# RetNet attention and SwiGLU feed-forward: how the first eight jobs turn q on TensorE

## The chip, the cores and the metric

The kernel runs on one core of one Trainium2 chip. A core has TensorE (PE in the profile, with its weight loads as PEld), VectorE (DVE), ScalarE (ACT), GpSimd (POOL) and SyncE (SP), which here issues nearly all transfers between HBM and SBUF. TensorE reads SBUF and writes PSUM, of which this kernel uses eight banks of 128 partitions by 512 float32 words. The metric is the device time of one execution in microseconds (us), as a median of several.

## The reference, cut to what matters

All data are float32. The first half is retention (linear attention with a decay) for 8 batches of 8 heads, 576 positions and 64 values per head; the second is a normalisation and a SwiGLU feed-forward over the 4608 rows that come out of it.

```python
scores = scale * np.matmul(q, k.transpose(0, 1, 3, 2))
Dmat = np.where(rel >= 0, gamma[:, None, None] ** rel[None, :, :], 0.0)
attn = np.matmul(scores * Dmat[None], v)
x = attn.transpose(0, 2, 1, 3).reshape(B * S, H * D)
xn = x / rms * rms_g
g, val = xn @ w_gate, xn @ w_val
out = (g * (1.0 / (1.0 + np.exp(-g))) * val) @ w_out
```

## The kernel before

**Jobs.** The attention is cut into 32 jobs, a batch and a pair of heads each. A job needs q and k with the 64 head values on the partitions, head 0 of the pair on partitions 0 to 63 and head 1 on 64 to 127, whereas memory has the positions in the rows. Jobs 8 to 31 turn them on VectorE (`prepare`, line 257). Jobs 0 to 7 turn them on TensorE, in the function `turn` (lines 220 to 250), which the change edits.

**What `turn` does.** It works on three PSUM banks. For q, the 512 first positions come as `d["q"]`, 128 partitions by 2 heads by 4 chunks by 64 values. For each of the four chunks and each of the two heads, the 128 by 64 piece is the stationary operand of a matrix product with the 128 by 128 identity `ident` as the moving one (line 234). `side(e)` is partitions 64e to 64e+63, so the product of head 0 lands in the upper half of the bank and that of head 1 in the lower, in every fourth column. For k both heads lie side by side, and a chunk is turned by one `nc.tensor.transpose` of 128 by 128 (line 228). ScalarE then copies each bank to SBUF (`qT`, `kT`, line 239). The 64 last positions of q and k are turned by two more transpositions of 64 by 128 (line 243) and copied too (line 250).

**What follows in a job.** `slot(j)` (line 404) issues on TensorE `values(j-1)` (line 355), `scores(j)` (line 285), `states(j)` (line 305) and `carried(j-1)` (line 375), all in products of 64 rows by 64 columns; on VectorE `weigh` (line 318, `ret`) and `sums` (line 334, `sum`). `states` needs v after `scale_v` on ScalarE (line 266).

**Order.** Every engine runs its own instructions in the order in which the program lists them. For the first part of the kernel that order is written out by hand in a string `PLAN`; `T` is `turn`, `S` is `slot`, `V` is `scale_v`, `Q` and `G` the squares for the normalisation, `N`, `D`, `X` the normalisation itself (`ms` line 454, `diag` line 468, `rb` line 519), `U` a block of the plain up projection of the first two row blocks (line 674), and `w` and `a` steps of a preparation of the weights on VectorE and ScalarE. It begins

```python
PLAN = """
    V0 T0 a1 a1 a1 S0 T1 V1 a1 S1 T2 V2 a1 a1 V3 w1 S2 w1 Q0 T3 Q1 a1 G0 S3 a1 a1 V4 T4 a1
    G1 a1 S4 a1 T5 a1 Q2 w1 G2 V5 w1 V6 Q3 S5 T6 a1 G3 a1 Q4 w1 V7 w1 S6 w1 F8 G4 N0 w1 a1
    a1 D0 a1 T7 w1 a1 a1 a1 a1 X0 S7 ...
```

The loads of these jobs are issued from SP's queue in the order of a list, before everything else: `load_first` (lines 170 and 178) for q, k and v, `load_tails` (line 188) for the last positions, with four blocks of weights among them (line 1034). Jobs 0 to 3 are loaded into the tile `h`, jobs 4 to 7 into `ring`. None of these loads waits for TensorE.

After the jobs of the plan, row blocks 2 to 8 follow in a loop, in which matrix products of the feed-forward (lines 614 and 779) fill TensorE and the remaining jobs are woven in.

Of the kernel before, what the change touches and what calls it, by code (L numbers as in the profile page):

```python
# [14 lines left out]
P = 128  # L15
# [26 lines left out]
def kernel(  # L42
# [11 lines left out]
    nc = tc.nc  # L54
    B, H, S, D = q.shape
# [31 lines left out]
    def bank(name):  # L87
        return banks.tile([P, 512], F32, tag="b", name=name)
# [13 lines left out]
    ident = const.tile([P, P], F32, name="ident")  # L102
# [107 lines left out]
    def warm_up(n, width=P):  # L210

        if not warm_of:
            warm_of[0] = bank("warm")
        for _ in range(n):
            nc.tensor.matmul(
                warm_of[0][:, :width], lhsT=ones, rhs=ones[:, :1].to_broadcast([P, width]),
                start=True, stop=True,
            )

    def turn(j):  # L220

        d = st[j]
        n = NFULL
        for nm in "qk":
            ps = bank(f"turn_{j}_{nm}")
            for c in range(n):
                if nm == "k":
                    nc.tensor.transpose(
                        out=ps[:, c * P : c * P + P],
                        in_=d["k"][:, c].rearrange("p e d -> p (e d)"), identity=ident,  # L230
                    )
                    continue
                for e in range(2):
                    nc.tensor.matmul(
                        ps[side(e), c : n * P : n], lhsT=d["q"][:, e, c], rhs=ident,
                        start=True, stop=True,
                    )
            t = d[nm + "T"] = att.tile([P, S], F32, tag=nm + "T", name=f"{nm}T_{j}")
            nc.scalar.copy(out=t[:, : n * P], in_=ps[:, : n * P])
        last = bank(f"turn_{j}_t")  # L240
        for i, nm in enumerate("qk"):
            o = slice(i * TAIL, i * TAIL + TAIL)
            nc.tensor.transpose(
                out=last[:, o], in_=d[nm + "t"].rearrange("p e d -> p (e d)"),
                identity=ident[:TAIL, :TAIL],
            )
        warm_up(j == 0, 2 * P)
        for i, nm in enumerate("qk"):
            o = slice(i * TAIL, i * TAIL + TAIL)
            nc.scalar.copy(out=d[nm + "T"][:, NFULL * P :], in_=last[:, o])  # L250
# [21 lines left out]
    def side(i):  # L272
        return slice(i * L, i * L + L)
# [922 lines left out]
    def start():  # L1196
# [12 lines left out]
        for i in (1, 0, 2):  # L1209
# [9 lines left out]
        }  # L1219
        tasks = {  # L1220
            "S": lambda j: slot(j, rest=j not in (0, FIRST)), "C": close, "T": turn, "V": scale_v,
            "P": prepare, "F": fetch, "Q": lambda j: squares.append(squared(*divmod(j, NHP))),
            "G": lambda j: gather(*squares.pop(0)), "N": norm_1, "D": diagonals, "X": norm_2,
# [83 lines left out]
```

## Time and profile before

| | us |
|---|---|
| median of 3 runs | 1109.53 |
| lowest and highest of them | 1109.16, 1113.54 |
| the profiled execution, its own time | 1110.56 |
| its span, first to last instruction | 1108.6 |
| TensorE busy in the span | 1090.6 |
| VectorE busy | 794.0 |
| GpSimd busy | 458.0 |
| ScalarE busy | 278.6 |

The profile is of one execution. Its span leaves 1.96 us of its own time outside. A matrix product in float32 is recorded as two instructions with a weight load each; a transposition as one. A line of a timeline has the start, the time from the first start to the last end, engine, line, what is written and read, the size of the stationary operand, the moving data, and a count; in brackets stands idle time ahead of it and what ended that. "issue" is waiting for which the profile shows no reason. The ends of matrix products are modelled, so starts are the safer measure. The eight calls of `turn` lie in the first 60 us, and the first plain up projection starts at 59.37 us.

### The profile page before, as it was taken

Reading aid. Unit: us, or ns where it says so; the run is one execution under the profiler, and the core shown is the slowest. Engines: PE = TensorE matmul, PEld = TensorE weight load, DVE = VectorE, ACT = ScalarE, POOL = GpSimd, SP = SyncE. Lnnn points to the kernel's source line nnn. Section 1 sums busy time; section 2 is a strip of 40 time slices with the busy share of each in tenths; the row PEclk is TensorE's granted clock in tenths of the full one; section 3 lists DMA queues with packets and bytes.
Section 4 is the critical chain, followed back from the end, with each engine's and each line's share of the span. In section 5 each row is a group of like instructions: output and inputs, shape, how many; then the busy total and the mean of one; then the engine's idle time right before and its main releaser. Section 6 shows DMA issues by size and latency. Waiting matters only on the chain.

```text
span 1108.6 us, 24401 instructions
## 1 busy us (share of the span) xinstructions
PE 1090.6 (98%) x10102; PEld 915.3 (83%) x10102; DVE 794.0 (72%) x1379; ACT 278.6 (25%) x565; POOL 458.0 (41%) x421
## 2 busy tenths in 40 slices
PE   8899999999999999999999999999999999999998
PEld 7754444479988899889988898889888998898888
DVE  4788578788867885778668785779476935594466
ACT  4665465211121311122022202131122111211110
POOL 0025335538430286026802482229311941393236
PEclk9899999999999999999999999999999999999999
DMA  7766798597978876897769965998475754585461
GB/s 182 204 198 222 261 267 217 198 342 187 289 269 219 201 262 222 203 230 226 268 191 206 283 251 157 242 240 290 146 207 200 266 204 169 179 288 165 152 247 41
DMA packets 253870, 243.72 MB, mean 220 GB/s; under 512 B 193088, under 2 KB 213824, under 8 KB 247616
## 3 DMA queue, kind: packets, MB, share of 16 engines
q1 hardware_dynamic: 252752, 241.87, 71.1%
q8 instruction: 79, 1.29, 0.5%
q10 hardware_dynamic: 1008, 0.30, 0.1%
q14 instruction: 31, 0.25, 0.1%
HBM read 212.05 MB, written 30.08 MB: 218 GB/s over the span
## 4 chain that ended last, share of the span: by engine, by line
PE 93%; DVE 3%; SPq 1%; ACT 1%; issue 1%; DMA 1%; POOL 0%; POOLq 0%; ACTq 0%; DVEq 0%
PE up L674 15%; PE x L614 13%; PE z L614 13%; PE w L614 13%; PE y L614 7%; PE xo L779 6%; PE xp L779 4%; PE zo L779 4%; PE zp L779 3%; PE yo L779 2%; PE wo L779 2%; PE av L355 2%; PE yp L779 2%; PE wp L779 2%; PE s L285 2%; PE av L375 1%
## 5 line engine op out<-in xcount | busy, mean ns | idle before, releaser
L674 PE MATMUL up<-x,ring 128*128 128x512 f32 x384 | 166.8, 594 | 0.0
L614 PE MATMUL x<-x,ring 128*128 128x256 f32 x672 | 160.8, 382 | 1.0 <-DVE t L698 1.0
L614 PE MATMUL w<-sums,ring 128*128 128x256 f32 x672 | 158.8, 379 | 0.0
L614 PE MATMUL z<-x,ring 128*128 128x256 f32 x672 | 158.7, 379 | 0.0
L736 POOL TENSOR_TENSOR vi<-h 128x384 f32<-128x384 f32 x32 | 39.9, 1248 | 277.0 <-DVE h L633 267.9
L674 PEld LDWEIGHTS up<-x,ring 128*128 128x128 f32 x384 | 72.4, 190 | 88.9 <-issue 85.6
L614 PEld LDWEIGHTS z<-x,ring 128*128 128x128 f32 x672 | 127.7, 190 | 19.9 <-issue 2.9
L614 PEld LDWEIGHTS w<-sums,ring 128*128 128x128 f32 x672 | 127.6, 190 | 17.4
L614 PEld LDWEIGHTS x<-x,ring 128*128 128x128 f32 x672 | 125.5, 190 | 18.2 <-issue 0.9
L741 POOL TENSOR_TENSOR vi<-h 128x384 f32<-128x384 f32 (+2 forms) x46 | 46.9, 1019 | 150.3 <-DVE h L633 150.3
L976 POOL TENSOR_TENSOR vi<-vi 128x512 f32<-128x512 f32 (+1 forms) x77 | 78.1, 1026 | 38.3 <-DVE vi L806 33.3
L640 ACT COPY m<-x 128x512 f32<-128x512 f32 x42 | 24.6, 586 | 230.4 <-PE x L614 230.4
L614 PE MATMUL y<-sums,ring 128*128 128x256 f32 x336 | 79.5, 379 | 1.5 <-DVE sums L533 1.5
L614 PEld LDWEIGHTS y<-sums,ring 128*128 128x128 f32 x336 | 63.7, 190 | 10.6 <-issue 2.0
L621 DVE TENSOR_TENSOR h<-u,w 128x512 f32<-128x512 f32 x42 | 28.9, 688 | 59.2 <-PE w L614 58.9
L621 DVE TENSOR_TENSOR u<-m,y 128x512 f32<-128x512 f32 x42 | 28.7, 684 | 47.9 <-PE y L614 47.8
L635 ACT ACTIVATE h<-h 128x512 f32<-128x512 f32 x63 | 39.7, 630 | 81.7 <-DVE h L621 81.7
L334 DVE SCALAR_TENSOR_TENSOR sum<-sum,gc,s 128x64 f32<-128x64 f32 x192 | 53.9, 281 | 6.8
L1096 POOL TENSOR_TENSOR vi<-vi 128x512 f32<-128x512 f32 (+1 forms) x24 | 40.3, 1681 | 36.9 <-DVE vi L1085 14.8
L741 POOL TENSOR_TENSOR vi<-vi,h 128x384 f32<-128x384 f32 (+2 forms) x46 | 47.9, 1042 | 3.6
L318 DVE SCALAR_TENSOR_TENSOR ret<-s,causal 128x320 f32<-128x320 f32 x64 | 28.5, 484 | 27.4 <-PE s L285 26.8
L1096 POOL TENSOR_TENSOR ring<-ring 128x512 f32<-128x512 f32 x24 | 30.5, 1275 | 42.1 <-DVE ring L1085 35.0
(310 smaller groups left out, 2050.3 us busy)
## 6 DMA issues: line engine op xcount, KB each, us to landing
ring<-w_out_blocks SPq DMA_DIRECT2D x59, 1344.0 KB, 6.6
ring<-w_up_blocks SPq DMA_DIRECT2D x42, 1792.0 KB, 7.9
w_out_blocks<-vi SPq DMA_DIRECT2D x21, 448.0 KB, 6.0
out_dram<-vi SPq DMA_DIRECT2D x64, 128.0 KB, 3.5
qraw<-in_q_dram SPq DMA_DIRECT2D x96, 72.0 KB, 5.2
kraw<-in_k_dram SPq DMA_DIRECT2D x96, 72.0 KB, 3.3
k<-in_k_dram SPq DMA_DIRECT2D x48, 128.0 KB, 3.1
v<-in_v_dram SPq DMA_DIRECT2D x48, 128.0 KB, 3.2
```

The costliest lines, as they stand in the source:

```text
L318: nc.vector.scalar_tensor_tensor(out=ret[:, e], in0=s[e][:, : n * L].rearrange("p (c k) -> p c k", k=L), scalar=float(_gamma(H)[2 * hp + e ...
L334: nc.vector.scalar_tensor_tensor(out=t[:, c], in0=t[:, c - 1], scalar=gc[:, hp : hp + 1], in1=part, op0=ALU.mult, op1=ALU.add,)
L614: nc.tensor.matmul(ps[:, i * HU : i * HU + HU], lhsT=w[:, PLACE[blk], c, i * P : i * P + P], rhs=t_of[u][blk][:, c], start=(start and i == ...
L621: nc.vector.tensor_tensor(out=o, in0=a, in1=pairs_of(ps), op=ALU.add)
L635: nc.scalar.activation(out=o, in_=c, func=AF.Silu)
L640: nc.scalar.copy(out=s1, in_=pairs_of(x_))
L674: nc.tensor.matmul(ps, lhsT=w[:, PLACE[blk], c % 2, i * P : i * P + P], rhs=x_of[u][:, c], start=(c == 0), stop=(c == NHP - 1),)
L736: eng.tensor_tensor(out=i1, in0=x12, in1=x11, op=ALU.subtract)
L741: eng.tensor_tensor(out=o[:, c], in0=a[:, c], in1=b[:, c], op=op)
L779: nc.tensor.matmul(ps, lhsT=lhs[:, c], rhs=w[:, s, c], start=((nm, s // 4) not in first), stop=False, skip_group_check=True,)
L976: eng.tensor_tensor(out=t[:, :, o], in0=t[:, :, x], in1=t[:, :, y], op=ALU.add)
L1096: nc.gpsimd.tensor_tensor(out=t[o], in0=t[x], in1=t[y], op=op)
```

## The change

In `turn`, head 0 of each chunk of q is turned by a transposition that writes partitions 0 to 63 of the bank; head 1 keeps its product with the identity. The order becomes head 0, head 1 for chunk 0, then for chunk 1 and so on, one of each kind in turn. Columns, banks, copies, the k part and the tails are as before, and so is every other function.

```diff
-                for e in range(2):
-                    nc.tensor.matmul(
-                        ps[side(e), c : n * P : n], lhsT=d["q"][:, e, c], rhs=ident,
-                        start=True, stop=True,
-                    )
+                nc.tensor.transpose(
+                    out=ps[:D, c : n * P : n], in_=d["q"][:, 0, c], identity=ident
+                )
+                nc.tensor.matmul(
+                    ps[side(1), c : n * P : n], lhsT=d["q"][:, 1, c], rhs=ident,
+                    start=True, stop=True,
+                )
```

## The prediction

> **What bounds the kernel now.** I read the page first, for the engine that ends last.
>
> ```profile
> PE 1090.6 (98%) x10102; PEld 915.3 (83%) x10102; DVE 794.0 (72%) x1379; ACT 278.6 (25%) x565; POOL 458.0 (41%) x421
> ...
> q8 instruction: 79, 1.29, 0.5%
> ...
> PE 93%; DVE 3%; SPq 1%; ACT 1%; issue 1%; DMA 1%; POOL 0%; POOLq 0%; ACTq 0%; DVEq 0%
> ```
>
> TensorE is busy for 1090.6 of 1108.6 us and makes up 93% of the chain. Of its 18 us of idle time some 10 lie before 59.4 us, where the edited function runs; the waits view after 60 us has about 5 us in all, the longest 1.5 (`y` for `sums`). So a microsecond added to TensorE before 59.4 us reaches the end, unless a wait in that stretch swallows it. Next, which instructions are concerned: the view of the tile `turn_q`, and that of line 228.
>
> ```profile
> L234 PE MATMUL turn_q<-ident,h x64: 272/273/476, 6.1 to 24.2; 128*64 128x128 f32 x64
> L234 PE MATMUL turn_q<-ident,ring x64: 272/273/474, 30.3 to 53.8; 128*64 128x128 f32 x64
> ```
> ```profile
> L228 PE MATMUL turn_k<-ident,h x16: 272/273/476, 8.0 to 24.8; 128*128 128x128 f32 x16
> ```
>
> Four jobs in `h` have 4 chunks x 2 heads = 32 products and 64 records: two passes each. Line 228 has 16 for 16 transpositions: one pass. The durations overlap, so prices come from starts, in the timeline of TensorE:
>
> ```profile
> 6.12 1.98 PE L234 MATMUL turn_q<-ident,h 128*64 128x128 f32 x16 [1.98 <-DMA h<-in_q_dram]
> 8.03 1.12 PE L228 MATMUL turn_k<-ident,h 128*128 128x128 f32 x4
> 9.07 0.47 PE L243 MATMUL turn_t<-ident,vi 64*128 64x64 f32 x2
> ...
> 12.41 1.09 PE L234 MATMUL turn_q<-ident,h 128*64 128x128 f32 x16
> 13.44 0.65 PE L228 MATMUL turn_k<-ident,h 128*128 128x128 f32 x4
> 14.02 0.34 PE L243 MATMUL turn_t<-ident,vi 64*128 64x64 f32 x2
> ...
> 30.31 0.62 PE L234 MATMUL turn_q<-ident,ring 128*64 128x128 f32 x6 [1.37 <-DVE sum L334]
> 33.20 1.54 PE L234 MATMUL turn_q<-ident,ring 128*64 128x128 f32 x10 [2.27 <-issue]
> ```
>
> The same view cut at 12.58 and at 12.69 us:
>
> ```profile
> 12.41 0.44 PE L234 MATMUL turn_q<-ident,h 128*64 128x128 f32 x4
> 12.41 0.55 PE L234 MATMUL turn_q<-ident,h 128*64 128x128 f32 x6
> ```
>
> Two more passes, one of each head, take one step of p = 0.11 us. So the heads' passes run side by side, and 16 passes are 8 steps. The q part takes 13.44 - 12.41 = 1.03 = 8p + 0.15, the k part 14.02 - 13.44 = 0.58 = 4p + 0.14. What is over, s = 0.145 us, is paid once at the end of each part, where the shape of the tile changes (128x64, 128x128, then 64x128). Within a part it isn't paid. In job 0 the same two equations, 1.91 = 8p + s and 1.04 = 4p + s, give p = 0.2175 and s = 0.17: half the clock.
>
> **What the Trainium skill says.** TensorEngine Tiling (Array Packing), Key Properties: "Changing tiling mode (not just tile) drains the TensorE", and tiles of one mode run in parallel. The trace agrees on both: s, and the two heads in one step. The same page, Gotcha 2: column tiling excludes the transpose mode for float32 input. So a transposition, though of 64 columns, takes the whole array. No instruction before is of this form, so the trace can't confirm it. TensorE: Matmul & The Clock Gate, Part 1: half clock until a window of about 3.4 us was busy, and again after an idle one. The trace agrees (0.2175 against 0.11), and the windows view shows a second such phase:
>
> ```profile
> 5.00:8.40 3.40, 2.28 (x18) 1.98 (x19) 0.00 (x0) 0.09 (x1) 0.00 (x0) 1.00 0.97 244
> 8.40:11.90 3.50, 3.50 (x52) 2.33 (x54) 0.00 (x0) 2.46 (x8) 0.00 (x0) 1.00 1.12 224
> 28.90:32.30 3.40, 0.66 (x8) 0.41 (x6) 3.11 (x11) 0.61 (x1) 0.00 (x0) 1.00 0.69 149
> 32.30:35.80 3.50, 2.60 (x15) 1.94 (x16) 0.00 (x0) 1.97 (x5) 0.00 (x0) 0.51 0.76 178
> 35.80:39.20 3.40, 3.40 (x113) 3.28 (x115) 0.49 (x1) 2.83 (x6) 0.09 (x1) 0.51 0.86 204
> ```
>
> Columns: stretch, length, busy PE, PEld, DVE, ACT, POOL, granted clock, DMA. (The clock's record begins at 11.9 us, so 1.00 ahead of it means nothing.) After 0.66 us of work in a window the clock halves at 32.3; after 2.60 of 3.50 it stays down; after a full window it returns at 39.2. Perfetto Trace Analysis, Transposes, advises transpositions over ordinary products; it says nothing of mixing them.
>
> **The change, part by part.** *Passes.* Per chunk, head 0 goes from two passes to one. That alone saves nothing: head 1 still needs two, and they set the length of the chunk, 2p. *Order.* Now transposition (whole array) and product (128x64) alternate, so each chunk has two changes of mode, and nothing lies beside anything: p + s + 2p + s = 3 x 0.11 + 2 x 0.145 = 0.62 us, four chunks 2.48 against 1.03. **+1.45 us per job** at full clock (the last s is the one paid now at the exit). At half clock 3 x 0.2175 + 2 x 0.17 = 0.99, four 3.97 against 1.91: **+2.06**. The bounds of this unseen mixture: 0 if the narrow transposition runs in the 128x64 mode, +1.45 if every change drains. I take the upper. ScalarE's copy of `turn_q` starts later by the same amount; behind it in ScalarE's queue wait the copy of `turn_k` and the scaling of v, and for these TensorE's scores and states, which shift with TensorE anyway. No DMA, bank or VectorE instruction is added.
>
> *Along the path.* Job 0: +2.06. It also puts drains into the window from 8.4 to 11.9, where now TensorE is busy throughout. Up to 10.2 us the array would stream 3 x 0.2175 of each 0.99, 66%, like the windows that weren't granted the clock (2.28 of 3.40 is 67%, 2.60 of 3.50 74%). I expect the grant one window later, at 15.3: states of job 0 at half clock (about +0.3) and the beginning of the next turn (+0.15). At T1 that is +2.5. Jobs 1 to 3: 3 x 1.45 = 4.35, sum 6.85. Of it waits for v disappear: 0.31 in job 2 (a bracket at 21.81, for ACT `h`), and in job 3 this one, in the chain of waits:
>
> ```profile
> 19.71 4.09 DMA h<-in_v_dram
> ...
> 23.82 0.51 ACT h L266
> ...
> 26.20 0.49 ACT kT L239
> ...
> 26.73 0.84 PE s L285 x39
> ```
>
> TensorE sat idle 0.65 us before 26.73 because ScalarE had waited for v of job 3 until 23.8. SP's loads don't move, so this cover goes once: 6.85 - 0.31 - 0.65 = 5.9 us late in the scores of job 3. VectorE's sums follow the scores and move with them.
>
> *Job 4* is the largest single term, and it has the other sign. Its turn stops at 30.93 for 2.27 us for "issue", and then runs at half clock to 39.2. The stop looks like a missing instruction: one packet of the instruction queue q8 lies between 30.5 and 31.0 us. At 1.29 MB in 79 packets, with 20204 instructions on TensorE, a packet would be 256 of these, somewhat less than a job. With TensorE 5.9 us later and slower in its turns, such a packet has longer to come, and the queue of loads that it shares the DMA engines with is shorter. I take the stop away, and the clock with it: 2.48 + 4.13 (a job from its k part to the next turn, 13.44 to 17.57) = 6.61 us where 30.31 to 40.19 was 9.88: -3.27, own drains included. The bounds: -3.27, and +2.06 if stop and half clock stay. Now late by 2.6.
>
> Job 5: +1.45, less a wait of 0.30 for v at 44.32. Job 6: +1.45. Job 7: +1.45, less the 0.64 that TensorE waits at 55.61 for `diag`, which doesn't hang on this turn. Sum 2.6 + 1.15 + 1.45 + 0.8 = **+6.0 us**. VectorE, busy for 6.4 of 6.8 us around 46 to 53, is the next engine in line, but its work resumes with the scores of job 4, less late than TensorE at the end. After 59.4 nothing gives back more than tenths.
>
> 1110.56 + 6.0 = 1116.6 us in the profiled execution's terms. That lies 1.03 above the median of the three runs, which spread over 4.4; I put the forecast at 1116.
>
> **The rivals.** *B: the stop in job 4 stays, or another comes, with half clock behind it.* For it: packets of instructions share the DMA engines with loads, and drains thin the work that keeps the clock up. Against it: the time per instruction grows. 5.9 + 2.06 + 3.4 = +11.4, 1121.5. *C: no change of mode.* The transposition of 64 columns takes the 128x64 tile of head 0 beside head 1's product. Then a chunk stays at 2p, and the only effect is 8 fewer instructions per job, 32 before job 4. Time 1110; if those 32 let the packet come in time, 3.3 less, 1107. It decides at one point: whether the step after a transposition costs p or p + s. Against it stands Gotcha 2. This case isn't slower. *A2: the clock of job 0 is granted at 11.9 as before.* Then jobs 0 and 1 lose 1.5 less, 1114.5.
>
> **How the numbers follow.** About 0.5%, 5.5 us, is what a measurement of this kernel tells from no change: slower begins at 1115.1. My forecast (with A2 as its lower part) 0.57, 1112 to 1119; B 0.28, 1119 to 1125; C 0.15. Slower: all of B and 0.6 of the first, 0.62. Faster: part of C, 0.06. Same: 0.32. The range 1111 to 1123 leaves out C and the end of B.
>
> **What would show it.** Right: q parts of about 2.5 us with 12 passes in warm jobs, starts of a transposition and of the next product about 0.25 apart; no "issue" of 2 us near 35 us; full clock from 15.3 on; the up projection starting near 65.4 instead of 59.37. Wrong: q parts of 1.03 us (C), a stop and a clock of 0.5 past 20 us (B), or a wait of TensorE after 60 us that shrinks by microseconds.

## The result and the profile after

The changed kernel takes 1116.68 us, median of 18 runs (1112.92 to 1121.15), beside 1109.28 us for the kernel before (18 runs, 1105.46 to 1113.54). The ratio is 1.0063, with a 95% interval of 1.0052 to 1.0075: slower by about 7 us. The forecast was 1116.

The profiled execution of the changed kernel took 1119.07 us (span 1117.1), 2.4 us above its median, and that of the kernel before 1110.56, 1.3 above its own. So the two traces differ by 8.5 us. The page after, busy engines and the chain of waits:

```profile
PE 1103.4 (99%) x10070; PEld 918.5 (82%) x10070; DVE 795.1 (71%) x1379; ACT 278.4 (25%) x565; POOL 458.3 (41%) x421
...
PE 96%; DVE 2%; ACT 1%; issue 1%; DMA 0%; POOL 0%; SPq 0%; POOLq 0%; ACTq 0%; DVEq 0%
```

TensorE has 32 records fewer (8 jobs x 4 products that are now one pass), yet is busy for 12.8 us more, and its share of the chain went up. The other engines work as before. The timeline of TensorE in job 2, at full clock, shows why:

```profile
20.59 0.30 PE L233 MATMUL turn_q<-ident,h 128*64 128x128 f32 x1
20.82 0.43 PE L236 MATMUL turn_q<-ident,h 128*64 128x128 f32 x2
21.18 0.30 PE L233 MATMUL turn_q<-ident,h 128*64 128x128 f32 x1
21.41 0.43 PE L236 MATMUL turn_q<-ident,h 128*64 128x128 f32 x2
...
22.96 0.66 PE L228 MATMUL turn_k<-ident,h 128*128 128x128 f32 x4
23.55 0.34 PE L245 MATMUL turn_t<-ident,vi 64*128 64x64 f32 x2
```

Line 233 is the transposition, line 236 the product. One chunk takes 21.18 - 20.59 = 0.59 us, the q part 22.96 - 20.59 = 2.37 (1.03 before), and the k part is as before (0.59; 0.58 before). The q parts alone add 8 x 1.34 = 10.7 us of TensorE time at full clock. The first up projection starts at 67.66 instead of 59.37 us. All but 0.2 us of the 8.5 has been lost by then.

The granted clock, in the windows view (length, busy PE, PEld, DVE, ACT, POOL, clock, DMA):

```profile
7.80:14.60 6.80, 6.80 (x88) 4.35 (x86) 1.40 (x5) 2.55 (x8) 0.00 (x0) 0.50 0.85 174
14.60:41.90 27.30, 25.15 (x636) 18.61 (x635) 17.64 (x60) 15.78 (x40) 0.36 (x4) 1.00 0.95 229
41.90:48.80 6.90, 6.90 (x130) 5.21 (x130) 3.70 (x7) 4.25 (x13) 0.09 (x1) 0.51 0.76 250
...
59.00:65.80 6.80, 6.80 (x70) 3.77 (x72) 3.68 (x7) 6.10 (x14) 0.36 (x2) 0.50 0.66 134
```

Three phases of 6.8 us at half clock, where the record of the kernel before has one (its start, before 11.9 us, is slow too, but outside the record). One follows another stop for "issue", in the `carried` part ahead of job 5:

```profile
37.94 0.91 PE L377 MATMUL av<-qT,sum 64*64 64x64 f32 x24
40.45 0.45 PE L377 MATMUL av<-qT,sum 64*64 64x64 f32 x8 [1.61 <-issue]
```

How late the changed kernel's execution is at each turn, from the starts in the two timelines, beside what the prediction's sum had there:

| start of | before, us | after, us | late by | forecast |
|---|---|---|---|---|
| turn 1 | 12.41 | 13.70 | 1.29 | 2.5 |
| turn 2 | 17.57 | 20.59 | 3.02 | 3.95 |
| turn 3 | 23.36 | 27.15 | 3.79 | 5.1 |
| turn 4 | 30.31 | 33.08 | 2.77 | 5.9 |
| turn 5 | 40.19 | 40.83 | 0.64 | 2.6 |
| turn 6 | 45.87 | 49.63 | 3.76 | 3.75 |
| turn 7 | 52.71 | 57.75 | 5.04 | 5.2 |
| up projection | 59.37 | 67.66 | 8.29 | 6.0 |

The medians fit (1116 forecast, 1116.68 measured), and several rows don't. The experiments ask two things: what makes the q part long, and how much of that length reaches the end.

### The profile page after: what moved, and what is told of

It is laid out like the page before. It is cut to its first block, busy times and chain, and to the rows that moved or that the text cites. A ratio compares the mean times of both kernels' runs of the same rounds, so it can differ in the third digit from the quotient of the medians.

```text
span 1117.1 us, 24332 instructions
## 1 busy us (share of the span) xinstructions
PE 1103.4 (99%) x10070; PEld 918.5 (82%) x10070; DVE 795.1 (71%) x1379; ACT 278.4 (25%) x565; POOL 458.3 (41%) x421
## 3 DMA queue, kind: packets, MB, share of 16 engines
q8 instruction: 79, 1.29, 0.5%
## 4 chain that ended last, share of the span: by engine, by line
PE 96%; DVE 2%; ACT 1%; issue 1%; DMA 0%; POOL 0%; SPq 0%; POOLq 0%; ACTq 0%; DVEq 0%
PE up L676 15%; PE x L616 13%; PE w L616 13%; PE z L616 13%; PE y L616 7%; PE xo L781 6%; PE xp L781 4%; PE zo L781 4%; PE zp L781 3%; PE yo L781 2%; PE wo L781 2%; PE av L357 2%; PE s L287 2%; PE av L377 2%; PE yp L781 2%; PE wp L781 2%
```

## The experiments

Each ratio is to the kernel before on the same chip, with its 95% interval.

### Grouped: four transpositions, then four products

```diff
-                for e in range(2): ...      # the products of before, for each c
+                if c:
+                    continue
+                for i in range(n):
+                    nc.tensor.transpose(out=ps[:D, i : n * P : n], in_=d["q"][:, 0, i], ...)
+                for i in range(n):
+                    nc.tensor.matmul(ps[side(1), i : n * P : n], lhsT=d["q"][:, 1, i], ...)
```

> The same instructions as in the changed kernel, but all four transpositions of head 0 first and then the four products of head 1: two changes of array mode per job instead of eight. Theory (the changes of mode cost about 0.13 to 0.145 us each, passes 0.11): q part at full clock 12 x 0.11 + 2 x 0.145 = 1.6 us (1.03 before, 2.37 in the changed kernel), ratio to before about 1.002 to 1.003. Rival 'a transposition in float32 is slow wherever it stands' (0.37 us more per chunk): q part about 2.4 us and ratio 1.006 as in the changed kernel. Rival 'only the lost side-by-side counts': q part 12 x 0.11 + 0.15 = 1.47, nearly the same as the theory, so the changed kernel itself speaks against it, not this run.

Measured: 1108.55 us, ratio 0.9989 (0.9979 to 0.9998). TensorE in job 6:

```profile
44.57 0.63 PE L236 MATMUL turn_q<-ident,ring 128*64 128x128 f32 x4
45.12 1.09 PE L240 MATMUL turn_q<-ident,ring 128*64 128x128 f32 x8
46.14 0.66 PE L228 MATMUL turn_k<-ident,ring 128*128 128x128 f32 x4
```

The q part is 46.14 - 44.57 = 1.57 us. So a transposition isn't slow in itself: the same instructions in another order take 0.8 us less per job. And a longer q part of +0.54 us per job, 4.3 in all, cost nothing at the end. That was not expected.

### Pairs: two transpositions, two products, and again

```diff
+                if c % 2:
+                    continue
+                for i in (c, c + 1): ...    # two transpositions of head 0
+                for i in (c, c + 1): ...    # two products of head 1
```

> Between the changed kernel and the grouped one: two transpositions, two products, and the same again; four changes of mode per job. Theory (0.11 per pass, 0.13 to 0.145 per change): q part 12 x 0.109 + 4 x 0.14 = 1.87 us, +0.84 per job or 6.7 us in all; some 3.6 us of waits hide it, as in the grouped run (4.4 us added, nothing lost), so ratio about 1.001 to 1.003. Rival 'the loss is proportional to the changes of mode': half of the change's loss, 1.003, and the grouped run would have shown 1.002.

Measured: 1110.71 us, ratio 1.0011 (1.0001 to 1.0021). Job 4:

```profile
30.16 0.41 PE L236 MATMUL turn_q<-ident,ring 128*64 128x128 f32 x2
30.50 0.65 PE L240 MATMUL turn_q<-ident,ring 128*64 128x128 f32 x4
31.08 0.41 PE L236 MATMUL turn_q<-ident,ring 128*64 128x128 f32 x2
31.42 0.65 PE L240 MATMUL turn_q<-ident,ring 128*64 128x128 f32 x4
32.00 0.66 PE L228 MATMUL turn_k<-ident,ring 128*128 128x128 f32 x4
```

The q part is 1.84 us. Grouped, pairs and the changed kernel have the same 12 passes and 2, 4 and 8 changes of mode (the exit counted): 1.57, 1.84 and 2.37 us. From 2 to 4 changes each costs 0.135 us, from 4 to 8 each 0.1325; what is left is 1.30 us, 0.109 for a pass. The price of a change of mode is shown, and in these three points it is a straight line.

### Products first, the transpositions beside those of k

```diff
+                for i in range(n):
+                    nc.tensor.matmul(ps[side(1), i : n * P : n], lhsT=d["q"][:, 1, i], ...)
+                for i in range(n):
+                    nc.tensor.transpose(out=ps[:D, i : n * P : n], in_=d["q"][:, 0, i], ...)
```

> The four products of head 1 first, then the four transpositions of head 0, right ahead of the transpositions of k, which have the same array mode: no change of mode is added at all, one stands elsewhere. Theory: from the first start of the q part to the first start of the tail's transpositions 8 x 0.11 + 0.145 + 8 x 0.11 + 0.145 = 2.05 us (before 1.61, changed kernel 2.96), ratio about 1.002. Rival 'a transposition is slow wherever it stands': 1.61 + 4 x 0.37 = 3.1 us, ratio 1.006.

Measured: 1107.91 us, ratio 0.9985 (0.9975 to 0.9996). Job 5:

```profile
41.58 1.09 PE L236 MATMUL turn_q<-ident,ring 128*64 128x128 f32 x8
42.60 0.63 PE L241 MATMUL turn_q<-ident,ring 128*64 128x128 f32 x4
43.06 0.60 PE L228 MATMUL turn_k<-ident,ring 128*128 128x128 f32 x4
43.59 0.34 PE L249 MATMUL turn_t<-ident,vi 64*128 64x64 f32 x2
```

From q to the tail 43.59 - 41.58 = 2.01 us, as expected (2.05). Between lines 241 and 228 there is no step: the four passes of line 241 take 43.06 - 42.60 = 0.46 us. So a transposition of 64 columns is of one mode with those of 128, which the prediction could only assume. This version has 0.40 us more TensorE work per job than the kernel before and is yet the only one, with the grouped one, that is faster than both kernels by its interval, if by 0.11 and 0.15% only. Where that comes from is taken up under what stays open.

### No transposition, heads one after the other

```diff
-                for e in range(2): ...      # for each c
+                if c:
+                    continue
+                for e in range(2):
+                    for i in range(n):
+                        nc.tensor.matmul(ps[side(e), i : n * P : n], lhsT=d["q"][:, e, i], ...)
```

> Products with the identity alone, as before, but all four of head 0 first and then all four of head 1, so that the heads no longer run side by side; no transposition and no added change of mode. Theory: 16 passes in a row, q part 16 x 0.11 + 0.15 = 1.9 us, ratio about 1.004; so the lost side-by-side would be dearer than the grouped transpositions. Rival 'the cost of the change is the transposition's own': q part stays near 1.03, ratio 1.000.

Measured: 1108.7 us, ratio 1.0000 (0.9990 to 1.0011). Job 6:

```profile
45.54 1.58 PE L237 MATMUL turn_q<-ident,ring 128*64 128x128 f32 x16
47.05 0.66 PE L228 MATMUL turn_k<-ident,ring 128*128 128x128 f32 x4
```

The q part is 1.51 us, not 1.9: 16 passes in some 12 steps, so four passes of the second head still ran beside the first. The rival, a q part of 1.03, falls; so does my size. +0.48 us per job again cost nothing that shows.

### A dense filler of the same length

```diff
+            if nm == "q":
+                for width in (512, 256):
+                    nc.tensor.matmul(ps[side(1), :width], lhsT=d["q"][:, 1, 0],
+                                     rhs=ones[:, :1].to_broadcast([P, width]), ...)
             for c in range(n): ...          # the products of before
```

> Products for both heads as before, but ahead of them a dense filler in the same array mode that writes rows which the products then overwrite: two more products of 512 and 256 moving columns, 4 passes, 1.3 us per job, so that the q part is as long as in the changed kernel (2.35 us) with no added change of mode. Theory A (only the length of the q part counts): ratio 1.006 as for the changed kernel. Theory B (alternating modes leaves the array idle half of the time and so costs the clock as well): full clock in nearly all runs (1.0, against a spread of 0.991 to 1.0), ratio about 1.004.

Measured: 1116.57 us, ratio 1.0065 (1.0050 to 1.0080), with a clock of 0.997 to 1.0 over six runs. Job 5:

```profile
42.28 0.64 PE L228 MATMUL turn_q<-ones,ring 128*64 128x512 f32 x1
...
44.60 0.66 PE L234 MATMUL turn_k<-ident,ring 128*128 128x128 f32 x4
```

2.32 us, with no added change of mode, and the same loss as the change (1.0063). So a dense filler of the same length costs as much as the alternation, and the smaller loss of theory B doesn't appear. Its clock does: none of these six runs is below 0.997, where six of the 18 of the changed kernel are at 0.994 or less. At a mean clock of 1.0 the filler takes 1115.05 us (two runs) and the change 1114.4 (five). Theory A, that the length alone counts, isn't shown: the pairs above (6.5 us added, 1.2 lost) and the change in four jobs below (5.4 added, 4.6 to 5.4 lost) don't go by length.

### The change in four jobs only

```diff
-                for e in range(2): ...      # the products of before
+                if j < 4:                   # or j >= 4, or j % 2 == 0
+                    nc.tensor.transpose(...)
+                for e in range(1 if j < 4 else 0, 2): ...
```

> The change in jobs 0 to 3 alone; jobs 4 to 7 turn q by products as before. Theory (the added time is hidden where TensorE waits for loads and for its next packet of instructions, and these waits stand around jobs 2 to 4): 4 x 1.34 = 5.4 us are added, 0.3 + 0.7 us of waits for v, 1.4 for q of job 4 and 2.3 of the stop in job 4 are there to hide them: ratio 0.999 to 1.001. Rival 'every job loses the same': half of the change's loss, 1.003.

> The change in jobs 4 to 7 alone. Theory: the same 5.4 us of TensorE time, but only about 0.6 + 0.3 us of waits to hide them, and the stop in job 4 stays: ratio 1.004. Rival 'every job loses the same': 1.003, and equal to the run with jobs 0 to 3.

> The change in jobs 0, 2, 4 and 6 alone: the same 4 x 1.34 = 5.4 us of added TensorE time and the same number of changes of mode as in the two runs of four jobs each (1.0049 and 1.0042), but spread evenly. Theory 'some 3 us of waits hide added time wherever it is spread': 2.4 us, ratio 1.001 to 1.003, as the pairs (6.7 us added, 1.0011) suggest; the clumped halves would be dearer for being clumped. Rival 'alternating single transpositions and products is dearer than its length': ratio 1.004 to 1.005 again.

Measured: jobs 0 to 3 1114.13 us, ratio 1.0049 (1.0033 to 1.0064); jobs 4 to 7 1113.46 us, 1.0042 (1.0026 to 1.0057); even jobs 1113.55 us, 1.0041 (1.0027 to 1.0054). My theory of the place falls: the early jobs, where the waits stand, lose as much as the late ones. That the waits hide time wherever it is spread falls too. The halves don't add up either: 1.0049 and 1.0042 against 1.0063 for both. Half of the change costs two thirds to three quarters of the whole. Part of that comes from behind the turns, as is shown under what stays open.

### Without the loads of q and k for three jobs

```diff
+        if j > 4:
+            d["q"], d["k"] = st[4]["q"], st[4]["k"]
+        else:
             nc.sync.dma_start(...)          # q; and k likewise
```

> The kernel before without the loads of q and k for jobs 5, 6 and 7 (1.5 MB); these jobs turn the q and k of job 4 instead, so their results are not the reference's, while every instruction of TensorE is as before. Theory (TensorE's stops for 'issue' after 448 + 256 n of its instructions are packets of instructions that queue behind the loads): the stops of over 1 us in jobs 4 and later are gone or under 0.5 us, the half-clock phases that follow them too; ratio about 0.997. Rival (the stops don't hang on these loads): stops of 1 to 2.5 us at the same counts, ratio 1.000.

> The changed kernel with the same loads left out (jobs 5, 6 and 7 turn the q and k of job 4). Theory: with fewer stops to hide it, more of the 10.7 us of added TensorE time is seen: 8 to 9 us above the run of the kernel before without these loads, ratio to the kernel before 1.004 to 1.005. Rival (stops don't hang on these loads): as the changed kernel, 1.006.

> The change in jobs 0 to 3 alone, with the same loads left out. Its run with all loads lost 1.0049 where 1.000 was expected, with three stops of 0.8 to 2.1 us for 'issue' after job 4. Theory (these stops, moved to later places, are why): stops gone, 2 to 4 us above the run of the kernel before without these loads, ratio about 1.000. Rival (the time of jobs 0 to 3 isn't hidden whatever follows): 5.4 us above it, ratio about 1.002; if stops don't hang on the loads, 1.005.

Measured: on the kernel before 1108.6 us, ratio 0.9989 (0.9976 to 1.0002); on the changed kernel 1120.63 us, 1.0096 (1.0077 to 1.0115); with the change in jobs 0 to 3 1115.42 us, 1.0055 (1.0040 to 1.0069). The timeline of the first of them, from 27 us on the lines with a stop for "issue":

```profile
28.77 0.40 PE L360 MATMUL av<-ret,h 64*64 64x64 f32 x12 [1.31 <-issue]
...
32.78 0.87 PE L239 MATMUL turn_q<-ident,ring 128*64 128x128 f32 x10 [0.98 <-issue]
...
37.62 1.09 PE L380 MATMUL av<-qT,sum 64*64 64x64 f32 x30 [1.23 <-issue]
...
43.63 0.27 PE L290 MATMUL s<-qT,kT 64*64 64x64 f32 x1 [1.74 <-issue]
```

The stops are all there, more of them than with the loads, so the rival is right on them: they don't hang on these loads. The loss did grow. With all loads the change costs 7 us of the 10.7 that it adds; without these loads it costs 1120.63 - 1108.6 = 12.0, and the change in jobs 0 to 3 costs 6.8, of 5.4 added. That waits for loads had hidden part of the change is not shown by this, for more is lost than was added. The clock is the nearer cause: five of the six runs of the changed kernel without these loads have a mean clock of 0.994 or less, with all loads six of 18 have, and these six have a median of 1119.5 us, near the 1120.63 here. For jobs 0 to 3 the interval overlaps the one with all loads.

### Both heads by one transposition

```diff
-        d["q"] = room[:, :n].rearrange("p (e t d) -> p e t d", e=2, d=D)
+        d["q"] = room[:, :n].rearrange("p (t e d) -> p t e d", e=2, d=D)
...
+                nc.tensor.transpose(out=ps[:, c : n * P : n],
+                    in_=d["q"][:, c].rearrange("p e d -> p (e d)"), identity=ident)
```

> q is loaded with the two heads side by side for each chunk, so that one transposition of 128 by 128 turns both heads, as for k. q and k parts are then of one mode with 8 single passes. Theory: from the first start of the q part to that of the tail's transpositions 8 x 0.11 + 0.145 = 1.02 us (1.61 before), 0.6 us less per job; if two thirds of it reach the end, as of the changed kernel's loss, 3 us, ratio 0.997. Rival: the load of q in pieces of 256 bytes instead of 1024 takes longer and the first jobs wait for it: ratio 1.000 or above, with waits of the q part for its load.

Measured: 1116.39 us, ratio 1.0060 (1.0038 to 1.0082). Job 3, and the waits of TensorE up to 66 us:

```profile
25.93 0.66 PE L233 MATMUL turn_q<-ident,h 128*128 128x128 f32 x4
26.42 0.60 PE L228 MATMUL turn_k<-ident,h 128*128 128x128 f32 x4
26.95 0.34 PE L242 MATMUL turn_t<-ident,vi 64*128 64x64 f32 x2
```
```profile
PE av L374 <- issue: 3.2, 1, 3.2
PE turn_q L233 <- DMA h<-in_q_dram: 2.2, 1, 2.2
PE turn_k L228 <- DMA h<-in_k_dram: 2.0, 1, 2.0
PE s L284 <- ACT kT L238: 1.9, 2, 1.6
```

The turn is as short as expected, 26.95 - 25.93 = 1.02 us, but TensorE waits 2.0 us for k, 1.9 for a copy and 3.2 for "issue", and its clock is halved for 17 us of this execution. Less work on the busiest engine made the kernel 0.6% slower. All six runs have a mean clock of 0.994 or less. The trace of the kernel before has 6.8 us at half clock on record, so the clock alone can make up about (17 - 6.8) / 2 = 5 us, an estimate from the two traces, of the 5.7 by which their spans differ. That the load in smaller pieces is to blame fits the wait for k, but it wasn't tried alone, and why the clock fell is open.

## Why the prediction was right, and where its sum was not

**The price of the alternation** was right, and shown. A chunk took 0.59 us (0.62 forecast), a job +1.34 (1.45), mostly because a change of mode costs 0.133 us and not 0.145. At half clock a chunk of job 1 took 14.67 - 13.70 = 0.97 us (0.99). Rival C, no change of mode, falls with the first lines of the timeline. The forecast that the saved passes buy nothing holds as well: head 1's two passes are the length of a chunk when they run beside head 0.

**The clock of job 0** came near the forecast, but the reason given for it isn't shown. In the five profiles in which job 0 alternates, full clock comes to stay between 13.5 and 16.5 us (15.3 forecast, 14.6 in the changed kernel). In the nine others it does so anywhere between 9.4 and 15.6, in five of them after 14.3. So drains need not be what delays it. Turn 1 starts at 13.70 to 14.61 us where job 0 alternates, and at 11.74 to 13.04 in the others. In the profiled execution of the changed kernel the clock happened to be up from 4.4 to 7.8 as well, which made job 0 cheaper there: 1.29 us late, not 2.5.

**The cover ahead of job 4 was read wrongly.** The prediction took the bracket `[1.37 <-DVE sum L334]` at 30.31 at its word and let the sums move with TensorE. The load of q for job 4, in the trace of the kernel before (SP's timeline, then the load by itself, its last figure the time from issue to landing):

```profile
23.70 0.47 SPq L170 DMA_DIRECT2D ring<-in_q_dram  x1
```
```profile
ring<-in_q_dram SPq DMA_DIRECT2D x1, 256.0 KB, 6.5
```

It landed at 23.70 + 6.5 = 30.2 us, just ahead of the turn. The turn waited for its own data, which don't move. The changed kernel confirms it. There the turn starts in the midst of VectorE's sums of job 3, with no bracket, so it doesn't wait for them:

```profile
32.88 1.86 DVE L336 SCALAR_TENSOR_TENSOR sum<-sum,gc,s 128x64 f32<-128x64 f32 x6
33.08 0.30 PE L233 MATMUL turn_q<-ident,ring 128*64 128x128 f32 x1
```

Lateness falls from 3.79 to 2.77. This is the term that was mis-sized: the sum let waits of 0.31 + 0.65 us go before job 4. In the trace the 0.65 went, and the 1.37 ahead of turn 4 as well, while the 0.31 for v stayed (0.29 at 25.60 us). At turn 4 that is 2.77 instead of 5.9, and 1.2 of the difference are job 0's.

**The stop in job 4** did go from its place, and turn 5 starts only 0.64 us late (2.6 forecast). But it came back at 40.45 us, with half clock after it: turn 5 to turn 6 takes 8.80 us where it took 5.68. A third half-clock phase, from 59.0 to 65.8, takes 9.91 us from turn 7 to the up projection instead of 6.66. So rival B was partly true of this execution: the sign that the prediction had set for it, a stop and a clock of 0.5 past 20 us, is there, and full clock from 15.3 us on is not. The two errors, cover too small and clock too kind, cancel at turn 7 (5.04 against 5.2); at the up projection the trace is 2.3 us later than the sum. That the forecast came within 0.7 us of the median is in part luck. How much the clock matters can be seen from the runs: the five of the changed kernel with a mean clock of 1.0 have a median of 1114.4 us, the six with 0.994 or less one of 1119.5.

**What stays open.** The loss is no straight function of the added time. Spread over all jobs, 3.2 us (beside k), 3.8 (heads in turn) and 4.3 us (grouped) cost nothing, 6.5 (pairs) 1.2 us, 10.3 (filler) and 10.7 (the change) 7. Yet 5.4 us in four jobs cost 4.6 to 5.4.

One part of this lies behind the turns. From the first up projection on, TensorE runs the same instructions in every version. Set side by side there, the traces keep step, but for single jumps of 0.15 to 2 us, each where one of two traces compared stands at a count of 448 + 256 n instructions (see the last section). Versions with fewer instructions in the turns reach these counts at other products. The kernel before, the grouped one and the change in even jobs, at the same place or just behind it:

```profile
352.48 0.34 PE L375 MATMUL av<-qT,sum 64*64 64x64 f32 x7 [1.24 <-issue]
```
```profile
350.78 0.67 PE L381 MATMUL av<-qT,sum 64*64 64x64 f32 x32
```
```profile
355.91 1.46 PE L618 MATMUL y<-sums,ring 128*128 128x256 f32 x6 [1.76 <-issue]
```

From the first up projection to the end the kernel before takes 1049.2 us, the changed one 1049.4, beside k, pairs and grouped 1048.1, 1047.7 and 1047.5, the change in four jobs 1050.2 to 1051.0. So 2 to 3.5 us between the small additions and the change in four jobs arise behind the turns, and not from the length of the q part. These are single traces, and no run changed the number of instructions alone.

Another part is the clock. Among runs with a mean clock of 1.0 the kernel before has a median of 1106.9 us (15 runs), beside k 1107.6 (16), grouped 1107.7 (11), heads in turn 1108.6 (12), pairs 1109.6 (9). There each is slower than before, by 0.7 to 2.7 us, and they gain by having such runs more often: 16 of 22 beside k, 7 of 59 for the kernel before beside them. Why a little more work of this kind keeps the clock up was not tried. What is left of the loss in four jobs is open.

## What to carry to other kernels

Count the changes of array mode in a stream of small products, not the passes: here one change cost more than a whole pass of 128 columns, and sorting the same instructions by mode took back all of the loss. Before a step on the busiest engine is priced at its full length, look up which loads the stretch waits for, and check what a bracket names against the landing times. A change in the number of instructions can move stops hundreds of microseconds further on. In the first tens of microseconds, stops and the clock move by as much as the change does, so a single trace there is one draw of several.

## What the runs showed of the hardware that was not expected

Stops for "issue" of 0.6 us and over recur at fixed counts: counted in the traces, TensorE had begun 704, 960, 1216, 1472, 1728, 1984 or 2240 of its instructions (matrix and weight-load records and waits for semaphores), 448 + 256 n. Each of the fourteen traces has at least one in the turns. The kernel before stopped after 1216 for 2.5 us, the changed one after 1472 for 1.8, start to start. This fits packets of 256 instructions that come late, the size that the prediction worked out from the 79 packets of queue q8. What delays them is open.

Passes of the second head began while the first head still had passes to come, though the program lists all of the first head's ahead: 16 passes took 1.51 us, not 16 x 0.109 = 1.74. The kernel before has the like, where the first scores of job 1 start ahead of products of `values`, which `slot` lists first:

```profile
14.81 0.27 PE L285 MATMUL s<-qT,kT 64*64 64x64 f32 x2
14.86 0.23 PE L355 MATMUL av<-ret,vi 64*64 64x64 f32 x2
```

That every engine runs its instructions in the listed order, as said at the beginning, is thus not strict for TensorE.

TensorE's recorded busy time says little of what keeps the clock. In the changed kernel the first window is busy throughout, with products of one moving column and the first chunks of job 7, and the clock was halved at its end. In the kernel before the second, with job 7 and a wait, is busy for 2.76 us of 3.40, and the clock stayed:

```profile
55.60:59.00 3.40, 3.40 (x37) 2.75 (x33) 3.08 (x13) 1.04 (x3) 0.73 (x1) 1.00 0.00 0
```
```profile
52.80:56.20 3.40, 2.76 (x24) 1.86 (x24) 3.12 (x12) 3.35 (x9) 1.02 (x1) 1.00 0.02 5
```

So the rule that the prediction used, that a busy window keeps the clock and an idle one loses it, doesn't hold for recorded busy time here.
